# A decode step of cached attention beside a gated MLP: keys in eight-head tiles, values in halves

## The chip, the cores and the metric

The kernel runs on one core of a Trainium2 chip, with nothing on the other cores. The metric is device time in microseconds for one execution, as the median of several runs. A profile of one execution shows where the time goes.

## The reference

One token for each of four batches is normalised; the result feeds an attention over a long cache and a small gated MLP, and both are added to the input.

```python
def _A_ref(x, k_cache, v_cache, wq, wo):      # x: (4, 1, 640); caches: (4, 32, 4096, 128), bf16
    q = (x @ wq).reshape(B, Sq, Hq, Dh).transpose(0, 2, 1, 3)
    scores = jnp.einsum('bhqd,bhkd->bhqk', q, k_cache) * Dh ** (-0.5)
    p = _softmax(scores, axis=-1)
    o = jnp.einsum('bhqk,bhkd->bhqd', p, v_cache)
    return o.transpose(0, 2, 1, 3).reshape(B, Sq, Hq * Dh) @ wo

xn = _layernorm(x, axis=-1)
return x + _A_ref(xn, A_k_cache, A_v_cache, A_wq, A_wo) + _B_ref(xn, B_w_in, B_w_sp, B_b_sp, B_w_out)
```

`_B_ref` projects to 1728 columns, applies gelu, normalises one half, scales and shifts it with `w_sp` and `b_sp`, multiplies by the other half and projects back. The key and value caches are 134 MB each; everything else together is some 14 MB.

## The kernel before

**Tiles.** Work goes tile by tile through the caches. A tile is four heads of one batch: 4 x 4096 rows of 128 numbers, laid over 128 partitions (lanes), so that each lane holds 128 consecutive rows, 32 KB in one run. There are 32 key tiles and 32 value tiles of 4 MB. Eight groups of four heads (`HG`) hold four tiles each, one for each batch.

**Places.** The pool `kv` has five slots of 32 KB a lane. The three first occupants are the two parts of `wq` and the GMLP weights `w_sb`; keys and values then take the slots in the order of the list `loads` (k0, k1, v0, k2, v1, k3, ...). `pump` issues the next loads on SyncE's (SP's) queue when the occupant of the slot five loads earlier is marked as used. The projection weights `wo` have a pool of their own (two buffers, eight blocks of four heads, loaded by `load_wo`; the last in pieces).

**Scores.** A query row is spread over the lanes (`stage_q`). `product(i, half)` multiplies half a key tile by it in place on VectorE (L463); `fold_half` adds the upper 64 columns to the lower (L472); `sums` has TensorE add the 64 columns down to eight through eight matmuls with the identity (L481); `row_sums` (VectorE, L492) adds the eight. Then `lane_max`, `lay_max` (ScalarE), `spread_max` (TensorE), `head_max` and `exps` make the exponents. These five, and `row_sums` of the second half, stand in the next tile's turn, after its first product.

**Values.** The end of `exps` (GpSimd, L539) spreads the probabilities of a tile over the columns of their heads, into one of four `p_m` buffers. `blocks` (L554) multiplies them with the values, 32 matmuls a tile, the two tiles of a pair adding up in `pv_acc`; after the second, ScalarE copies the sum (L564) and `gather` (L575) picks out each head. At the end of a group `group_den`, `group_norm`, `group_turn`, `group_pick` and `group_proj` divide by the denominators and add the group's projection to `out_ps`. The last value tile comes in four pieces, the last three handled by `pairs` (L587).

The order on TensorE, VectorE, ScalarE and SyncE is the order in which the program text is written (`manual_schedule`); GpSimd runs its own list in order. `gmlp` runs whole before the first key tile.

Of the kernel before, what the change touches and what calls it, by code (L numbers as in the profile page):

```python
# [15 lines left out]
KV_SLOTS = 5  # L16
EXTRA_K = (24, 28)
# [4 lines left out]
def kernel(  # L22
# [26 lines left out]
    HT = 4  # L49
# [4 lines left out]
    HC = NC // 2  # L54
    HD2 = Dh // 2
    RW = 8
    SLOT = NC * Dh
# [4 lines left out]

# [5 lines left out]
    kv = ctx.enter_context(tc.tile_pool(name="kv", bufs=KV_SLOTS))  # L68
    wop = ctx.enter_context(tc.tile_pool(name="wop", bufs=2))
# [10 lines left out]
    def slot(name):  # L80
        return kv.tile([P, SLOT], BF16, tag="kv", name=name)


# [4 lines left out]
    wq_v = A_wq.rearrange("(p c) n -> p c n", c=DC)  # L88
    wq_parts = []
    for c0, c1 in ((0, HT), (HT, DC)):  # L90
        t = slot("wq")[:, 0 : (c1 - c0) * HD].rearrange("p (c n) -> p c n", n=HD)
        nc.sync.dma_start(out=t, in_=wq_v[:, c0:c1, :])  # L92
        wq_parts += [(t, i) for i in range(c1 - c0)]
# [6 lines left out]
    w_sb = slot("w_sb")  # L100
    w_in_sb = w_sb[:, 0 : DC * F].rearrange("p (c n) -> p c n", c=DC)
    w_out_sb = w_sb[:, DC * F : DC * F + NFC * D].rearrange("p (k n) -> p k n", k=NFC)
    nc.sync.dma_start(out=w_in_sb, in_=B_w_in.rearrange("(p c) n -> p c n", c=DC))
    nc.sync.dma_start(  # L104
        out=w_out_sb[:, 0:NFF, :], in_=B_w_out[0 : NFF * P].rearrange("(p k) n -> p k n", k=NFF)
    )
    nc.sync.dma_start(out=w_out_sb[:FT, NFF, :], in_=B_w_out[NFF * P : Fh])

    def kv_view(cache, i):
        hg, b = divmod(i, Bsz)  # L110
        return cache[b, HT * hg : HT * (hg + 1)].rearrange("h s d -> (h s) d").rearrange(
            "(p c) d -> p (c d)", c=NC
        )

    k_tiles, v_tiles = {}, {}
    V_CUTS = (0, 64, 96, 112, NC)

    def load(which, i):
        cache, tiles = (A_k_cache, k_tiles) if which == "k" else (A_v_cache, v_tiles)
        t = slot("k_nat" if which == "k" else "v_nat")  # L120
        cuts = V_CUTS if (which, i) == ("v", NT - 1) else (0, NC)
        for c0, c1 in zip(cuts, cuts[1:]):
            if c0 == V_CUTS[1]:
                load_wo(HG - 2)
            nc.sync.dma_start(  # L125
                out=t[:, c0 * Dh : c1 * Dh], in_=kv_view(cache, i)[:, c0 * Dh : c1 * Dh]
            )
        tiles[i] = t[:].rearrange("p (c d) -> p c d", d=Dh)

    loads = [("k", 0), ("k", 1)]  # L130
    n_k = 2
    for i in range(NT):
        loads.append(("v", i))
        for _ in range(2 if i + 1 in EXTRA_K else 1):
            if n_k < NT:
                loads.append(("k", n_k))
                n_k += 1
    occupants = [("w", 0), ("w", 1), ("w", 2)] + loads
    used = set()
    n_loaded = [0]  # L140

    def pump():
        while n_loaded[0] < len(loads):
            at = n_loaded[0] + 3 - KV_SLOTS
            if at >= 0 and occupants[at] not in used:
                return
            load(*loads[n_loaded[0]])
            n_loaded[0] += 1

# [5 lines left out]
    def load_wo(j):  # L155
        wo_tiles[j] = wop.tile([P, HT, D], BF16, name="wo")
        if j == HG - 1:
            for hh in range(HT):
                cuts = (0, D) if hh < HT - 1 else (0, NOH, D)
                for n0, n1 in zip(cuts, cuts[1:]):  # L160
                    nc.sync.dma_start(
                        out=wo_tiles[j][:, hh, n0:n1], in_=wo_h[j][:, hh, n0:n1]
                    )
            return
        nc.sync.dma_start(out=wo_tiles[j][:].rearrange("p r n -> p (r n)"), in_=wo_r[j])

    pump()


# [9 lines left out]
    head_scale = const.tile([P, P], FP32)  # L179
    nc.vector.memset(head_scale[:], 0.0)  # L180
# [7 lines left out]
    for hh in range(HT):  # L188
        ps = slice(hh * LN, (hh + 1) * LN)
        nc.vector.memset(head_scale[ps, ps], scale_qk)  # L190
# [3 lines left out]
    GC = 4  # L194
    CG = P // LN
    assert 2 * GC * HT == LN and GC * Dh * 4 <= 2048
    pv_acc = ps_acc.tile([P, GC * Dh], FP32)
    sel = const.tile([P, GC, HT, 2], FP32)
    for e in range(2):
        nc.vector.tensor_reduce(  # L200
            out=sel[:, :, :, e],
            in_=ident_f[:].rearrange("p (g e k h) -> p e k h g", g=CG, e=2, k=GC)[:, e],
            axis=AX.X,
            op=ALU.add,
        )

    hmask = const.tile([P, HT], FP32)
    nc.vector.memset(hmask[:], 0.0)
    for hh in range(HT):
        nc.vector.memset(hmask[hh * LN : (hh + 1) * LN, hh : hh + 1], 1.0)  # L210
# [7 lines left out]


# [8 lines left out]

    place = const.tile([P, HT, HT * Bsz], BF16)
    nc.gpsimd.memset(place[:], 0.0)  # L230
    for hh in range(HT):
        nc.gpsimd.tensor_copy(
            out=place[:, hh, hh * Bsz : (hh + 1) * Bsz], in_=lane_diag[:, 0:Bsz]
        )
# [5 lines left out]


    p_m = [const.tile([P, NC // GC, LN], BF16, name=f"pm{b}") for b in range(Bsz)]
    acc = [const.tile([P, Bsz], FP32, name=f"acc{g}") for g in range(NACC)]
    for t in p_m:
        nc.gpsimd.memset(t[:], 0.0)


# [25 lines left out]
    for c in range(DC):  # L273
# [5 lines left out]
    xnT = const.tile([P, DC, LN], BF16)  # L279
# [3 lines left out]
    q_sb = const.tile([P, HG // CG, HT * Dh], BF16)  # L283
    q_ps = [
        ps_m.tile([P, HT * Dh], FP32, tag="m", name="q_ps") for _ in range(HG // CG)
    ]
    for c in range(DC):
        t, i = wq_parts[c]
        for hg in range(HG):
            g = hg % CG  # L290
            nc.tensor.matmul(  # L291
                out=q_ps[hg // CG][g * LN : (g + 1) * LN, :],
                lhsT=xnT[:, c, :],
                rhs=t[:, i, hg * HT * Dh : (hg + 1) * HT * Dh],
                start=(c == 0),
                stop=(c == DC - 1),
            )
    nc.vector.tensor_copy(out=q_sb[:, 0, :], in_=q_ps[0][:])  # L298
    nc.scalar.copy(out=q_sb[:, 1, :], in_=q_ps[1][:])

# [26 lines left out]
    def gmlp():  # L329
        zz, gw, gt, gz, sq = (gm[n] for n in ("zz", "gw", "gt", "gz", "sq"))  # L330
        zT = ps_pv.tile([P, 2, NFC, Bsz], FP32, tag="pv", name="zT")
        for t in range(2):
            f1 = t * Fh + NFF * P
            w_t = w_in_sb[:, :, t * Fh : f1].rearrange("p c (f k) -> p c k f", k=NFF)
            for k in range(NFC):
                for c in range(DC):
# [6 lines left out]
                    )  # L343
        nc.vector.tensor_copy(out=zz[:, :, 0:NFF, :], in_=zT[:, :, 0:NFF, :])
# [93 lines left out]
    sums_ps, maxes = {}, {}  # L438

    def stage_q(hg):  # L440
        g, ps = hg % CG, slice(hg % CG * LN, (hg % CG + 1) * LN)
        qr_ps = ps_m.tile([HT * Bsz, Dh], FP32, tag="m", name="qr_ps")
        for hh in range(HT):
# [3 lines left out]
                rhs=q_sb[ps, hg // CG, hh * Dh : (hh + 1) * Dh],  # L447
                start=(hh == 0),
                stop=(hh == HT - 1),
# [11 lines left out]
    def product(i, half):  # L461
        t = k_tiles[i][:, half * HC : (half + 1) * HC, :]
        nc.vector.tensor_tensor(  # L463
            out=t,
            in0=t,
            in1=qbcs[i // Bsz][:, i % Bsz, None, :].to_broadcast([P, HC, Dh]),
            op=ALU.mult,
        )

    def fold_half(i, half):  # L470
        t = k_tiles[i][:, half * HC : (half + 1) * HC, :]
# [4 lines left out]
    def sums(i, half):  # L476
        t = k_tiles[i][:, half * HC : (half + 1) * HC, :]
# [298 lines left out]
```

## Time and profile before

| what | value |
|---|---|
| median of 3 runs | 663.85 us (663.52 to 676.66) |
| profiled execution, its own time | 663.97 us |
| its span in the profile | 662.2 us |
| TensorE, VectorE, ScalarE, GpSimd busy | 53%, 74%, 7%, 23% |
| bytes read from HBM | 282.24 MB, 426 GB/s over the span |
| mean granted TensorE clock | 0.713 |

The profile shows one execution. Its lines give groups of instructions by source line and engine, as busy time, mean duration, and the idle time before them with what ended it. The windows give busy times by stretch of time, with the share of time in which the 16 DMA engines carried packets. Tiles carry the names of the program's buffers.

### The profile page before, as it was taken

Reading aid. Unit: us, or ns where it says so; the run is one execution under the profiler, and the core shown is the slowest. Engines: PE = TensorE matmul, PEld = TensorE weight load, DVE = VectorE, ACT = ScalarE, POOL = GpSimd, SP = SyncE. Lnnn points to the kernel's source line nnn. Section 1 sums busy time; section 2 is a strip of 40 time slices with the busy share of each in tenths; the row PEclk is TensorE's granted clock in tenths of the full one; section 3 lists DMA queues with packets and bytes.
Section 4 is the critical chain, followed back from the end, with each engine's and each line's share of the span. In section 5 each row is a group of like instructions: output and inputs, shape, how many; then the busy total and the mean of one; then the engine's idle time right before and its main releaser. Section 6 shows DMA issues by size and latency. Waiting matters only on the chain.

```text
span 662.2 us, 5116 instructions
## 1 busy us (share of the span) xinstructions
PE 353.6 (53%) x2109; PEld 147.0 (22%) x2109; DVE 491.3 (74%) x334; ACT 49.4 (7%) x138; POOL 151.3 (23%) x57
## 2 busy tenths in 40 slices
PE   2526563646446555664445645465653756435567
PEld 1402221212113221221212212121211312112123
DVE  2289797767769777787776797776787899777950
ACT  0201100001000010001000010000100000000010
POOL 3002222012222012222112222112222133122230
PEclk9999766776755677766778665777576577688586
DMA  9999999999999999999999999999999999999997
GB/s 368 426 416 442 439 418 440 428 434 443 424 431 432 432 442 426 436 430 426 443 428 434 434 424 441 432 431 434 426 438 439 424 442 420 433 443 422 433 430 288
DMA packets 12115, 282.57 MB, mean 427 GB/s; under 512 B 1360, under 2 KB 2108, under 8 KB 3388
## 3 DMA queue, kind: packets, MB, share of 16 engines
q1 hardware_dynamic: 12072, 282.25, 99.2%
q8 instruction: 16, 0.26, 0.1%
q14 instruction: 7, 0.06, 0.0%
q10 hardware_dynamic: 20, 0.01, 0.0%
HBM read 282.24 MB, written 0.01 MB: 426 GB/s over the span
## 4 chain that ended last, share of the span: by engine, by line
issue 49%; DMA 25%; POOL 15%; DVE 7%; PE 3%; SPq 1%; ACT 0%; POOLq 0%; DVEq 0%; ACTq 0%
DMA k_nat<-in_A_k_cache_dram 20%; POOL pm L539 15%; DMA v_nat<-in_A_v_cache_dram 4%; DVE k_nat L463 4%; DVE k_nat L472 2%; PE s_ps L481 2%; PE pv_acc L554 1%; DVE s_sb L492 0%; SPq L125 0%; PE out_ps L653 0%; PE pv L575 0%; SPq L104 0%; POOL own_sum L599 0%; DVE m L501 0%; SPq L92 0%
## 5 line engine op out<-in xcount | busy, mean ns | idle before, releaser
L463 DVE TENSOR_TENSOR k_nat<-k_nat,qbc 128x8192 bf16<-128x8192 bf16 x64 | 282.8, 4419 | 96.2 <-DMA k_nat<-in_A_k_cache_dram 96.2
L539 POOL TENSOR_TENSOR pm<-p,hmask_bf 128x512 bf16<-128x512 bf16 x32 | 142.4, 4451 | 491.7 <-ACT p L530 491.7
L481 PE MATMUL s_ps<-k_nat,ident 128*128 128x512 bf16 x512 | 194.0, 547 | 67.2 <-DVE k_nat L472 67.2
L472 DVE TENSOR_TENSOR k_nat<-k_nat 128x4096 bf16<-128x4096 bf16 x64 | 151.8, 2372 | 0.0
L554 PE MATMUL pv_acc<-v_nat,pm 128*32 128x512 bf16 x1008 | 87.6, 508 | 39.8 <-POOL pm L539 36.2
L514 PE MATMUL max_ps<-lay,head_scale 128*128 128x32 f32 x64 | 19.1, 390 | 167.0 <-ACT lay L507 167.0
L481 PEld LDWEIGHTS <-ident 128*128 128x128 bf16 x512 | 69.7, 138 | 173.8 <-issue 158.8
L514 PEld LDWEIGHTS max_ps<-lay,head_scale 128*128 128x128 f32 x64 | 14.9, 290 | 182.1 <-ACT lay L507 182.1
L554 PEld LDWEIGHTS <-pm 128*32 128x32 bf16 x1008 | 30.0, 118 | 95.8 <-POOL pm L539 52.9
L492 DVE TENSOR_REDUCE s_sb<-s_ps 128x64 f32<-128x512 f32 x64 | 43.3, 677 | 4.3 <-PE s_ps L481 4.3
L507 ACT ACTIVATE lay<-lane_diag,m 128x32 f32<-128x32 f32 x32 | 10.3, 321 | 397.5 <-DVE m L501 397.5
L608 DVE RECIPROCAL rden<-den 128x16 f32<-128x16 f32 x8 | 2.1, 258 | 34.1 <-PE den L606 34.1
L575 PE MATMUL pv<-sel,pv_sb 128*128 128x8 f32 x128 | 20.6, 288 | 8.4 <-ACT pv_sb L564 8.4
L575 PEld LDWEIGHTS pv<-sel,pv_sb 128*128 128x128 f32 x128 | 19.1, 229 | 15.5 <-ACT pv_sb L564 15.5
L530 ACT ACTIVATE p<-s_sb,nb 128x128 bf16<-128x128 f32 x32 | 12.8, 402 | 63.5 <-DVE nb L521 63.5
L564 ACT COPY pv_sb<-pv_acc 128x512 f32<-128x512 f32 x16 | 9.4, 586 | 92.2 <-PE pv_acc L554 92.2
L501 DVE TENSOR_REDUCE m<-s_sb 128x1 f32<-128x128 f32 x32 | 9.1, 286 | 1.1
L291 PE MATMUL q_ps<-wq,xnT 128*32 128x512 bf16 x40 | 4.5, 630 | 8.7 <-DMA wq<-in_A_wq_dram 8.7
L653 PE MATMUL out_ps<-wo,o_r 128*4 128x320 bf16 x56 | 8.1, 437 | 0.0
L298 DVE CAST q_sb<-q_ps 128x512 bf16<-128x512 f32 x1 | 0.7, 692 | 9.7 <-PE q_ps L291 9.7
L613 DVE TENSOR_TENSOR o_n<-pv,rden 128x16 bf16<-128x16 f32 x8 | 1.3, 168 | 7.7 <-PE pv L587 7.7
L521 DVE TENSOR_REDUCE nb<-max_ps 128x1 f32<-128x32 f32 x32 | 5.9, 183 | 0.9 <-PE max_ps L514 0.9
(94 smaller groups left out, 90.4 us busy)
## 6 DMA issues: line engine op xcount, KB each, us to landing
k_nat<-in_A_k_cache_dram SPq DMA_DIRECT2D x32, 4096.0 KB, 37.2
v_nat<-in_A_v_cache_dram SPq DMA_DIRECT2D x31, 4096.0 KB, 33.5
wo<-in_A_wo_dram SPq DMA_DIRECT2D x7, 640.0 KB, 38.3
wq<-in_A_wq_dram SPq DMA_DIRECT2D x1, 4096.0 KB, 13.1
w_sb<-in_B_w_in_dram SPq DMA_DIRECT2D x1, 2160.0 KB, 19.7
v_nat<-in_A_v_cache_dram SPq DMA_DIRECT2D x1, 2048.0 KB, 24.5
wq<-in_A_wq_dram SPq DMA_DIRECT2D x1, 1024.0 KB, 15.0
v_nat<-in_A_v_cache_dram SPq DMA_DIRECT2D x1, 1024.0 KB
```

The costliest lines, as they stand in the source:

```text
L463: nc.vector.tensor_tensor(out=t, in0=t, in1=qbcs[i // Bsz][:, i % Bsz, None, :].to_broadcast([P, HC, Dh]), op=ALU.mult,)
L472: nc.vector.tensor_tensor(out=t[:, :, 0:HD2], in0=t[:, :, 0:HD2], in1=t[:, :, HD2:Dh], op=ALU.add)
L481: nc.tensor.matmul(out=s[:], lhsT=ident[:], rhs=t[:, :, g * RW : (g + 1) * RW], start=(g == 0), stop=(g == n - 1),)
L492: nc.vector.tensor_reduce(out=scores[i][:, half * HC : (half + 1) * HC], in_=sums_ps.pop((i, half))[:], axis=AX.X, op=ALU.add,)
L501: nc.vector.tensor_reduce(out=m1[:], in_=scores[i][:], axis=AX.X, op=ALU.max)
L507: nc.scalar.activation(out=d[:], in_=lane_diag[:], func=ACT.Copy, scale=maxes[i][:, 0:1])
L514: nc.tensor.matmul(out=ps[:], lhsT=head_scale[:], rhs=maxes[i][:], start=True, stop=True)
L530: nc.scalar.activation(out=p[:], in_=scores.pop(i)[:], func=ACT.Exp, bias=nb[:], scale=scale_qk, accum_out=acc[hg % NACC][:, b : b + 1],)
L539: nc.gpsimd.tensor_tensor(out=p_m[b][:, :, e : e + GC * HT].rearrange("p g (c h) -> p g c h", h=HT), in0=p[:].rearrange("p (g c) -> p g c" ...
L554: nc.tensor.matmul(out=pv_acc[g * LN : (g + 1) * LN, :], lhsT=pm[:, c // GC, :], rhs=v_nat[:, c : c + GC, :].rearrange("p c d -> p (c d)") ...
L564: nc.scalar.copy(out=pv_sb[:], in_=pv_acc[:])
L575: nc.tensor.matmul(out=pvs[hg][:, :, b - 1 : b + 1], lhsT=pv_sb[:, k * Dh : (k + 1) * Dh], rhs=sel[:, k, :, :], start=(k == 0), stop=stop ...
```

## The change

A tile becomes eight heads of one batch (`HT = 8`): 256 rows a lane, 64 KB in one run, 16 tiles of keys and 16 of values, four groups. Vector and matrix work on keys goes by quarters (`NQ = 4`), each as large as a half was.

The five slots become one tile, `ring`, of five units of 32 KB. A key tile takes two neighbouring units (a pair, units 2 and 3 for even tiles, 0 and 1 for odd ones) with one load of 8 MB; the first key tile comes in two loads. A value tile comes as two halves of 32 KB a lane: the first goes to the unit of the first half of the same tile's keys, once these are summed, the second to unit 4. The GMLP weights begin in unit 4; their matmuls (`gmlp_in`) stand in the first tile's third quarter, the rest (`gmlp_out`) behind its softmax. For the last three tiles the value halves have other units, written out by hand. The loads stand in a list with their units; `pump` issues the next one when all that was in its units is marked as used, and is called after `sums`, `blocks` and `group_proj`. `wo` has four blocks, one buffer, 10 KB a lane each; the last comes in five pieces after the last values.

The softmax of a tile, from the last `row_sums` to `exps`, stands at the end of its own turn, not in the next (except for the last tile but one). Probabilities are spread by `deal`, twice a tile, 1024 elements a lane each, into one of two `p_m` buffers. `blocks` now runs by halves of a tile: the first half of the tile before in the first quarter of a turn, the second in the third; `gather` follows each tile.

```diff
-    HT = 4
+    HT = 8
-    HC = NC // 2
+    UC = NC // 2
+    NQ = 4
+    QC = NC // NQ
-    kv = ctx.enter_context(tc.tile_pool(name="kv", bufs=KV_SLOTS))
-    wop = ctx.enter_context(tc.tile_pool(name="wop", bufs=2))
+    kv = ctx.enter_context(tc.tile_pool(name="kv", bufs=1))
+    wop = ctx.enter_context(tc.tile_pool(name="wop", bufs=1))
...
+    def load_k(i):
+        t = units(pair(i), 2)
+        step = (1 if i == 0 else 2) * UNIT
+        for e in range(0, 2 * UNIT, step):
+            nc.sync.dma_start(out=t[:, e : e + step], in_=run_view(A_k_cache, i)[:, e : e + step])
...
+    plan_k(0)
+    plan("w", SOLO, 1, load_w)
+    plan_k(1)
+    for i in range(NT - 3):
+        plan_v(i, 0, pair(i))
+        plan_v(i, 1, SOLO)
+        if i % Bsz == 0 and i // Bsz < HG - 1:
+            plan(("wo", i // Bsz), 0, 0, load_wo, i // Bsz)
+        plan_k(i + 2)
+    plan_k(NT - 1)
+    plan_v(NT - 3, 0, SOLO)
+    plan_v(NT - 3, 1, pair(NT - 2))
+    plan_v(NT - 2, 0, SOLO)
+    plan_v(NT - 2, 1, pair(NT - 2) + 1)
+    plan_v(NT - 1, 0, pair(NT - 2))
+    plan_v(NT - 1, 1, SOLO)
+    plan(("wo", HG - 1), 0, 0, load_wo, HG - 1)
...
+    def deal(i, part, engine):
+        g0, g1 = part * UC // GC, (part + 1) * UC // GC
+        engine.tensor_tensor(
+            out=p_m[i % 2][:, g0:g1, :].rearrange("p g (c h) -> p g c h", h=HT),
+            in0=probs[i][:, part * UC : (part + 1) * UC]
+            .rearrange("p (g c) -> p g c", c=GC)[:, :, :, None]
+            .to_broadcast([P, UC // GC, GC, HT]),
+            in1=hmask_bf[:, None, None, :].to_broadcast([P, UC // GC, GC, HT]),
+            op=ALU.mult,
+        )
...
+            for q in range(NQ):
+                product(i, q)
+                if q:
+                    row_sums(i, q - 1)
+                elif late is not None:
+                    row_sums(late, NQ - 1)
+                    lane_max(late)
+                fold(i, q)
+                if q == 0 and late is not None:
+                    exps(late)
+                    deal(late, 0, nc.gpsimd)
+                    deal(late, 1, nc.gpsimd)
+                sums(i, q)
+                if i == 0 and q == 2:
+                    gmlp_in()
+                if i % Bsz == Bsz - 1 and q == 1 and i // Bsz + 1 < HG:
+                    stage_q(i // Bsz + 1)
...
+                elif i:
+                    if q == 0:
+                        blocks(i - 1, 0)
+                    elif q == 2:
+                        blocks(i - 1, 1)
+                        gather(i - 1)
+                        if ends:
+                            group_den(i // Bsz - 1)
+            if ends:
+                group_norm(i // Bsz - 1)
+                group_turn(i // Bsz - 1)
+            if i != LAST - 1:
+                row_sums(i, NQ - 1)
+                lane_max(i)
+                if ends:
+                    group_pick(i // Bsz - 1)
+                exps(i)
+                deal(i, 0, nc.gpsimd)
+                deal(i, 1, nc.vector if i == LAST else nc.gpsimd)
+            if ends:
+                group_proj(i // Bsz - 1)
+            if i == 0:
+                gmlp_out()
+                used.add("w")
+                pump()
```

In the last two turns the `blocks` calls stand elsewhere (the second half of tile 13's values, for one, in the last turn's first quarter), and the last tile's second deal runs on VectorE.

## The prediction, put down before the run

> **What bounds the kernel now.** I read the page's DMA part first, because the diff rewrites the loads, then the windows, the groups by line, and the timelines of VectorE and GpSimd.
>
> ```profile
> span 662.2 us, 5116 instructions
> ...
> DMA  9999999999999999999999999999999999999997
> ...
> DMA packets 12115, 282.57 MB, mean 427 GB/s; under 512 B 1360, under 2 KB 2108, under 8 KB 3388
> ...
> q1 hardware_dynamic: 12072, 282.25, 99.2%
> ```
> ```profile
> 40.00:560.00 520.00, 285.23 (x1529) 114.02 (x1529) 410.82 (x242) 36.23 (x108) 121.76 (x33) 0.69 1.00 433
> ...
> 655.00:658.00 3.00, 1.99 (x65) 1.72 (x64) 0.03 (x1) 0.00 (x0) 0.00 (x0) 0.98 0.74 278
> 658.00:660.00 2.00, 1.27 (x8) 0.50 (x8) 0.62 (x2) 0.42 (x1) 0.00 (x0) 0.50 0.14 42
> ```
> The windows' columns are PE, PE weight load, DVE, ACT and POOL busy, the granted PE clock, DMA share, GB/s. From 40 to 560 us the 16 DMA engines are busy all the time (share 1.00) at 433 GB/s. The chain of waits calls half the span "issue" and puts GpSimd in it, but no engine there is full: the transfers set the pace, and all 282 MB stay in the change. Only three things can move: the transfers' own rate, gaps in the queue, and the ends.
>
> ```profile
> L463 DVE TENSOR_TENSOR k_nat<-k_nat,qbc 128x8192 bf16<-128x8192 bf16 x64 | 282.8, 4419 | 96.2 <-DMA k_nat<-in_A_k_cache_dram 96.2
> L539 POOL TENSOR_TENSOR pm<-p,hmask_bf 128x512 bf16<-128x512 bf16 x32 | 142.4, 4451 | 491.7 <-ACT p L530 491.7
> L481 PE MATMUL s_ps<-k_nat,ident 128*128 128x512 bf16 x512 | 194.0, 547 | 67.2 <-DVE k_nat L472 67.2
> L472 DVE TENSOR_TENSOR k_nat<-k_nat 128x4096 bf16<-128x4096 bf16 x64 | 151.8, 2372 | 0.0
> L554 PE MATMUL pv_acc<-v_nat,pm 128*32 128x512 bf16 x1008 | 87.6, 508 | 39.8 <-POOL pm L539 36.2
> L492 DVE TENSOR_REDUCE s_sb<-s_ps 128x64 f32<-128x512 f32 x64 | 43.3, 677 | 4.3 <-PE s_ps L481 4.3
> ```
> ```profile
> 90.78 4.41 DVE L463 TENSOR_TENSOR k_nat<-k_nat,qbc 128x8192 bf16<-128x8192 bf16 x1
> 95.11 0.68 DVE L492 TENSOR_REDUCE s_sb<-s_ps 128x64 f32<-128x512 f32 x1
> 95.71 2.52 DVE L472 TENSOR_TENSOR k_nat<-k_nat 128x4096 bf16<-128x4096 bf16 x1
> 102.88 4.43 DVE L463 TENSOR_TENSOR k_nat<-k_nat,qbc 128x8192 bf16<-128x8192 bf16 x1 [4.65 <-DMA k_nat<-in_A_k_cache_dram]
> ```
> ```profile
> 630.71 4.56 POOL L539 TENSOR_TENSOR pm<-p,hmask_bf 128x512 bf16<-128x512 bf16 x1 [10.37 <-ACT p L530]
> 644.49 1.04 POOL L539 TENSOR_TENSOR pm<-p,hmask_bf 128x512 bf16<-128x512 bf16 x1 [9.22 <-ACT p L530]
> ```
> VectorE waits for keys between tiles (4.65 us in the last DVE line). The same GpSimd multiply takes 4.56 us beside a running product and 1.04 us at 644.49, where VectorE is idle: its own work is 1.04 us, the rest is waiting for the product to end.
>
> **Part 1, the transfers (-1.2 us).** The trace's DMA packet records give one engine's packet as 1.213 us for 32 KB, 0.611 for 16 KB, 0.309 for 8 KB, 0.196 for 5,120 B. These lie on one line: 602 ns for each 16 KB and 9 ns a packet. A 64 KB key run is then 9 + 2408 = 2.417 us against 2 x 1.213. Each engine carries 8 lanes of each of the 16 key tiles: 128 pairs x 9 ns = 1.15 us saved. The nearest other row, a run cut into two packets all the same, saves 0. Projection weights: 7 blocks of 8 x 0.196 plus a last one in 1280 and 640 byte pieces (1.83) were 12.8 us; 3 of 8 x 0.385 plus a last one twice as large (3.66) are 12.9. `wq` in one 40 KB run, values in 32 KB runs: the same. Half the key issues on SP's queue fall away; SP is idle, nothing. I take -1.2.
>
> At this place a rule speaks for much more. The Trainium skill, page "DMA: Bandwidth & Descriptors" (Anatomy of one DMA), puts a fixed cost of some 2 us on each DMA beside its bytes. The trace does not show that cost here: with transfers queued behind one another the share is 1.00 at 433 GB/s. By the page 16 fewer key DMAs would take off some 32 us (an estimate), by the row nothing; it stands as a rival.
>
> **Part 2, the start (0).** Order on the queue: `wq` 12.1 us, first key tile 2 x 9.70, GMLP weights 7.8, second key tile 19.35, then values into the first tile's freed half. The slowest engine starts at about 3.5, so that values end at 3.5 + 12.1 + 19.4 + 7.8 + 19.35 + 9.7 = 71.9, or 72.7 with the 0.8 that the first key transfer lost beside those weights now. The next half needs the place of the GMLP weights, freed when `gmlp_out` is done. First keys at 25.6; four quarters of product 4.42, row sums 0.65 and fold 2.28 (the first without row sums) are 28.8, giving 54.4; sums 3.57, row sums, maximum, exponent, about 6 us, give 60.6; the GMLP chain took 8.1 us (25.26 to 33.40) and pays one more table load, 1.28: 70. First packets follow an issue by 1.0 us (0.74 to 1.77 at the start), 71 against 72.7: no gap. If the GMLP's small products wait for both deals, 2 to 4 us, the gap is up to 2.
>
> **Part 3, the ring (+0.3; bounds 0 and 27).** Five 32 KB places remain, but a key tile now claims two at once. Keys i+1 may only be issued when `blocks(i-1, 0)` has read the values in their first place. From the last packet of keys i: landing 0.35, product and fold 6.7, sums 3.03 (194.0/64), `blocks` 2.74 (87.6/32), issue 1.0: packets can flow at 13.8 to 14.1 (the values themselves land at 10.05), and the queue holds work until 19.4. So 5 us in hand; with both matmul groups at their slow 3.57 and 3.61, 4.2.
>
> The second question is whether a tile's chain fits into the period of 2 x 19.4 = 38.8 us. Before, the softmax of a tile lay under the next tile's first product; now `row_sums(i, 3)` to `exps(i)` run ahead of it, and VectorE waits: sums of the third quarter 21.4 to 24.4, `blocks` to 27.2, copy and gather 0.59 + 1.06, last sums to 31.9, then 0.65 + 0.41 + 0.33 + 0.63 + 0.2 = 34.1, exponent 34.7, both deals. A deal has 1024 elements a lane instead of 512: 2.08 us at twice the 1.04, lower bound 1.04, upper 4.56, the common row. 1.04 is its nearest row, since VectorE is idle just then. 35.1 + 2 x 2.08 = 39.2 against the next keys at 39.1: they just fit, and one product in some periods starts late by a microsecond, inside the 5 us. At the slow matmul durations the same chain ends at 41.2: 2.1 us a period if deals go first, 13 periods, 27 us; that is the upper bound. The mean rows are the ones that a mixed clock (0.69 in the window) gives, so I take 0.3, for one or two slips. Group ends (tiles 4, 8, 12) add den, turn and pick, 1 to 1.5 us; the 3.1 us of projection weights lie ahead of the key load after two of them.
>
> **Part 4, the end (+1.7; bounds 0 and 6).** The last packet lands at about 658.7 now and the span ends 3.5 later. In the new order the last tile's product starts some 51.6 before the last packet (behind the late values of tile 13): quarters 29.7, two deals in the windows 4, last sums 3.03, softmax 2.9, deal 2.1 and denominator 0.9 give -7.4 or so; `blocks` 2.74, half of it again, copy and gather 1.7, pairs 2.1, norm 0.4, sixteen projections 2.5: +2.5. Result copy and output 2.7: 5.2 after the last packet instead of 3.5. All matmuls fast: 0; all slow: +6.
>
> **Sum.** 662.2 - 1.2 + 0 + 0.3 + 1.7 = 663.0. The profiled execution took 663.97, 1.8 over its span; the median of three is 663.85, so the execution stands for it. 663.0 + 1.8 = 664.8.
>
> **Rivals.**
> *The run is still two packets* (the change does not do what it says): the saving of 1.2 is gone, 666.0. No packet in the trace is over 32 KB, so nothing speaks against it. Chance 0.08.
>
> *The ring runs dry, slower.* Place: the deals at the end of tile i against the first product of tile i+1. Once the two deals end over 4 us after the next keys landed (a deal over 3.5 us, or half clock throughout), keys i+1 come late each period. For it: L539's common 4.56 and matmul groups of 3.57; against: 1.04 without a product, and products that never exceed 4.43 now. Price: about 1 us x 14 periods, + 6 at the end - 1.2 = +19, 683. Chance 0.14. The Trainium skill, "SBUF — State Buffer" (Who interferes with whom), calls that shared port an exclusive lock held for the whole instruction; 4.56 against 1.04 agrees, and by it a deal that comes first holds up the whole product, 2.08 each.
>
> *Values read with gaps.* Halves of 32 KB now lie 64 KB apart in memory. If that slowed them to the 417 GB/s of the slowest early window (20 to 40 us) instead of 433, 134.2 MB take 321.8 instead of 309.9: +12, 677. Against: 32 KB packets are at 1.213 in nine of ten records. Chance 0.04. The Trainium skill, same DMA page (Latency and other measured facts), has a row pitch of 512 KiB cost some 3%; no run here shows a pitch beyond 32 KB.
>
> *A fixed cost per DMA goes* (the rule in part 1): 16 x 2 is the page's estimate; by rows a cost can hide only in the gap of 433 and the 443 of the best slices, 2.3% of 655: 15 us, 649. Chance 0.01, as share 1.00 speaks against it.
>
> **Numbers.** My forecast has 0.73, its own range 661.5 to 669. The range to 676 takes in the split run and the ring's milder slips; under 661.5 would need an end shorter than today's. Over 2% (about what a measurement of this kernel can tell from no change, 650.6 and 677.1) slower: the ring 0.13, half of the values 0.02, together 0.15; faster 0.01; within 0.84.
>
> **What would show it.** Right: key packets of 64 KB, share 1.00 and 433 GB/s in the middle, products waiting for keys and never SP's key issue for `blocks` while the queue is empty, deals near 2 us, and 5 us from last landing to the end. Wrong: DMA digits under 9 at a period of about 40 us, or `pm` rows of 4 us and more at tile ends, would give the ring; a middle under 430 GB/s at share 1.00 the spaced values. Above 677 or below 651 the reading "transfers set the time" is wrong.

## The result, and the profile after

The changed kernel takes 670.13 us (median of 6, 668.78 to 672.55) against 663.62 us for the kernel before (median of 6, three of them those of the table above): a ratio of 1.0098, 95% interval 1.0087 to 1.0109. It is slower by 6.5 us, 5.3 us above the predicted 664.8, and within the 2% that was named as no difference. It lies above the forecast's own range (661.5 to 669) and inside the wider one, to 676, that took in milder slips of the ring. The profiled execution is the quickest of the six, 668.78 us with a span of 666.8; the other five have spans of 667.3 to 670.5.

The page's head, DMA rows and queue:

```profile
span 666.8 us, 4747 instructions
...
DMA  9999899999999999999999999999999999999997
...
DMA packets 9873, 282.56 MB, mean 424 GB/s; under 512 B 1040, under 2 KB 2428, under 8 KB 2812
...
q1 hardware_dynamic: 9832, 282.25, 98.6%
```

The bytes are the same, in 2242 fewer packets, 1920 of them by key runs of 64 KB, but the share fell from 99.2% to 98.6% and one digit, the fifth (67 to 83 us), is below 9. The windows (PE, weight load, DVE, ACT and POOL busy, granted clock, DMA share, GB/s) show where:

```profile
71.00:73.00 2.00, 0.64 (x6) 0.14 (x3) 2.00 (x1) 0.00 (x0) 0.00 (x0) 0.50 0.87 250
73.00:557.00 484.00, 226.37 (x1396) 89.03 (x1399) 377.74 (x183) 21.75 (x55) 70.28 (x27) 0.69 1.00 432
557.00:560.00 3.00, 1.39 (x24) 0.55 (x17) 3.00 (x3) 0.00 (x0) 0.00 (x0) 0.95 1.11 382
560.00:618.00 58.00, 27.88 (x132) 10.31 (x132) 52.99 (x25) 1.80 (x5) 7.92 (x2) 0.68 0.97 417
618.00:620.00 2.00, 0.70 (x4) 0.34 (x4) 2.00 (x3) 0.55 (x2) 0.00 (x0) 1.00 0.86 279
```

The middle runs as before, 432 GB/s at share 1.00. Three short stretches do not: 71 to 73, 557 to 560 and 618 to 620 us. (A window counts a packet whole if it starts there. So in a short one the share can pass 1, and 560 to 618 us shows only 417 GB/s although the packet records have no gap between 561 and 616.) From the start and length of each packet in the trace's DMA records, the 16 engines stand idle, on the mean, 1.42, 1.64 and 0.35 us in the three; the packets around them run long by another 0.60, 0.69 and 0.44. That is 5.1 us. Less the 1.2 us that the longer runs were to save, and with 0.3 more at the end (last packet 662.98, end 3.8 behind it; before 658.68 and 3.5), 4.2 of the 4.6 us between the two spans are placed; the other 0.4 is spread thin. Some 0.2 to 0.3 us more lie outside the span: an execution of the changed kernel takes 1.98 to 2.12 us over its span, one of the kernel before 1.73 to 1.85.

**The first stretch.** The timeline there:

```profile
61.46 3.74 POOL L561 TENSOR_TENSOR pm<-p,hmask_bf 128x1024 bf16<-128x1024 bf16 x2 [52.18 <-ACT gt L380]
61.50 1.90 DVE L383 TENSOR_SCALAR gt<-gt 128x56 f32<-128x56 f32 x1 [0.32 <-ACT gt L380]
63.44 1.84 DVE L386 TENSOR_TENSOR gz<-zz,gt 128x56 f32<-128x56 f32 x1
69.61 2.03 PE L456 MATMUL out_ps<-ring,yT 128*4 128x320 bf16 x14 [0.92 <-DVE yT L452]
71.68 0.33 SPq L139 DMA_DIRECT2D ring<-in_A_v_cache_dram  x1
```

Two steps of the GMLP's gelu on VectorE take 1.90 and 1.84 us, each as long as one of the two deals that GpSimd runs beside them. The GMLP weights are read for the last time at 71.6, and the second half of the first values, which takes their place, is issued at 71.68. By then most of the 16 engines have run dry, from 70.9 us on; the new packets start at 72.6 to 73.5.

**The second stretch.** VectorE's waits (total, times, longest) and its timeline through tile 12:

```profile
DVE ring L495 <- DMA ring<-in_A_k_cache_dram: 46.2, 11, 6.2
DVE s_sb L527 <- PE s_ps L513: 43.3, 15, 3.7
DVE rden L626 <- PE den L624: 26.1, 4, 8.5
```
```profile
501.90 4.43 DVE L495 TENSOR_TENSOR ring<-ring,qbc 128x8192 bf16<-128x8192 bf16 x1 [5.86 <-DMA ring<-in_A_k_cache_dram]
506.36 2.29 DVE L504 TENSOR_TENSOR ring<-ring 128x4096 bf16<-128x4096 bf16 x1
508.57 4.42 DVE L495 TENSOR_TENSOR ring<-ring,qbc 128x8192 bf16<-128x8192 bf16 x1
...
530.50 0.36 DVE L626 RECIPROCAL rden<-den 128x32 f32<-128x32 f32 x1 [7.58 <-PE den L624]
530.78 4.36 DVE L495 TENSOR_TENSOR ring<-ring,qbc 128x8192 bf16<-128x8192 bf16 x1
...
543.87 4.42 DVE L495 TENSOR_TENSOR ring<-ring,qbc 128x8192 bf16<-128x8192 bf16 x1
548.32 3.86 DVE L504 TENSOR_TENSOR ring<-ring 128x4096 bf16<-128x4096 bf16 x1
552.11 6.11 DVE L495 TENSOR_TENSOR ring<-ring,qbc 128x8192 bf16<-128x8192 bf16 x1
```
```profile
496.81 3.74 POOL L561 TENSOR_TENSOR pm<-p,hmask_bf 128x1024 bf16<-128x1024 bf16 x2 [33.94 <-ACT p L550]
544.73 9.21 POOL L561 TENSOR_TENSOR pm<-p,hmask_bf 128x1024 bf16<-128x1024 bf16 x2 [43.97 <-ACT p L550]
580.18 7.92 POOL L561 TENSOR_TENSOR pm<-p,hmask_bf 128x1024 bf16<-128x1024 bf16 x2 [26.24 <-ACT p L550]
```

At a group end the reciprocal of the denominators, 0.36 us of work, stands ahead of the last product in VectorE's list, and its matmul stands behind `blocks` and `gather` on TensorE: VectorE stands still for 7.58 us. Tile 12 started on time (it had waited 5.86 us for its keys), but tile 13's product starts 42.0 us later, not 38.8. By then the deals of tile 12 no longer fall into the gap between tiles: they meet tile 13's first product and take 9.21 us instead of 3.74. By their times in the trace each waits for the one before: the first deal ends 1.7 us behind that product, the fold behind the first deal, the second deal behind the fold, the second product behind the second deal. Fold and product take 3.86 and 6.11 us instead of 2.28 and 4.42. The same happens behind the other two group ends (pairs of 9.21 us at 227.57 and 386.50). The tile after each is still late (7.92 us, the last row); at the other tile ends up to tile 11 the pair takes 3.74 or 3.75.

How far this delays the next transfer is read from what the key load waits for. The key loads behind tiles 12 and 13, and on TensorE the sums and `blocks` ahead of the second:

```profile
514.50 0.33 SPq L131 DMA_DIRECT2D ring<-in_A_k_cache_dram  x1
```
```profile
552.24 3.57 PE L513 MATMUL s_ps<-ring,ident 128*128 128x512 bf16 x8 [6.18 <-DVE ring L504]
555.74 2.65 PE L575 MATMUL pv_acc<-ring,pm 128*32 128x512 bf16 x32
558.45 0.33 SPq L131 DMA_DIRECT2D ring<-in_A_k_cache_dram  x1
```

Tile 14's keys wait for `blocks` to read the first half of tile 12's values, and that stands behind the sums of tile 13's first quarter. They are issued 43.95 us after tile 13's keys, 5.2 over the period: 3.2 from the late start, 1.6 from the held fold, 0.4 from a slower `blocks`. The held second product lies behind all this and adds nothing. The ring had some 5 us in hand for the slowest DMA engine, but the engines end their work up to 2 us apart: all but a few have run dry between 556.6 and 558.5 us, and the new packets start at 559.4 to 560.2.

### The profile page after: what moved, and what is told of

Same layout as the page of the kernel before. It is cut to its first block, busy times and chain, and to the rows that moved or that the text cites. A ratio compares the mean times of both kernels' runs of the same rounds, so it can differ in the third digit from the quotient of the medians.

```text
span 666.8 us, 4747 instructions
## 1 busy us (share of the span) xinstructions
PE 313.4 (47%) x2033; PEld 127.2 (19%) x2033; DVE 507.4 (76%) x278; ACT 34.3 (5%) x82; POOL 97.9 (15%) x60
## 3 DMA queue, kind: packets, MB, share of 16 engines
q1 hardware_dynamic: 9832, 282.25, 98.6%
## 4 chain that ended last, share of the span: by engine, by line
DMA 48%; DVE 34%; PE 17%; ACT 1%; issue 1%; SPq 0%; DVEq 0%; ACTq 0%
DMA ring<-in_A_k_cache_dram 41%; DVE ring L495 19%; DVE ring L504 11%; PE s_ps L513 10%; PE pv_acc L575 5%; DMA ring<-in_A_v_cache_dram 3%; DMA wo<-in_A_wo_dram 3%; DVE s_sb L527 2%; PE zT L363 1%; PE pv L593 0%; DVE gt L383 0%; PE max_ps L540 0%; DVE gz L386 0%; ACT pv_sb L589 0%; DVE m L536 0%
## 5 line engine op out<-in xcount | busy, mean ns | idle before, releaser
L495 DVE TENSOR_TENSOR ring<-ring,qbc 128x8192 bf16<-128x8192 bf16 x64 | 291.7, 4558 | 46.2 <-DMA ring<-in_A_k_cache_dram 46.2
L513 PE MATMUL s_ps<-ring,ident 128*128 128x512 bf16 x512 | 187.9, 533 | 284.0 <-DVE ring L504 284.0
L561 POOL TENSOR_TENSOR pm<-p,hmask_bf 128x1024 bf16<-128x1024 bf16 x31 | 93.5, 3035 | 548.6 <-ACT p L550 496.4
L504 DVE TENSOR_TENSOR ring<-ring 128x4096 bf16<-128x4096 bf16 x64 | 156.6, 2447 | 0.5
L513 PEld LDWEIGHTS <-ident 128*128 128x128 bf16 x512 | 63.9, 126 | 385.5 <-issue 320.0
L575 PE MATMUL pv_acc<-ring,pm 128*32 128x512 bf16 x1008 | 77.4, 462 | 0.9 <-DMA ring<-in_A_v_cache_dram 0.9
L540 PE MATMUL max_ps<-lay,head_scale 128*128 128x16 f32 x32 | 7.0, 294 | 23.4 <-ACT lay L538 23.4
L540 PEld LDWEIGHTS max_ps<-lay,head_scale 128*128 128x128 f32 x32 | 5.4, 211 | 30.6 <-ACT lay L538 30.6
L550 ACT ACTIVATE p<-s_sb,nb 128x256 bf16<-128x256 f32 x16 | 8.1, 508 | 12.3 <-DVE nb L546 12.3
L536 DVE TENSOR_REDUCE m<-s_sb 128x1 f32<-128x256 f32 x16 | 6.7, 420 | 0.5
```

What stands on the lines that cost most here:

```text
L495: nc.vector.tensor_tensor(out=t, in0=t, in1=qbcs[i // Bsz][:, i % Bsz, None, :].to_broadcast([P, QC, Dh]), op=ALU.mult,)
L504: nc.vector.tensor_tensor(out=t[:, :, 0:HD2], in0=t[:, :, 0:HD2], in1=t[:, :, HD2:Dh], op=ALU.add)
L513: nc.tensor.matmul(out=s[:], lhsT=ident[:], rhs=t[:, :, g * RW : (g + 1) * RW], start=(g == 0), stop=(g == n - 1),)
L536: nc.vector.tensor_reduce(out=m1[:], in_=scores[i][:], axis=AX.X, op=ALU.max)
L540: nc.tensor.matmul(out=ps[:], lhsT=head_scale[:], rhs=d[:], start=True, stop=True)
L550: nc.scalar.activation(out=p[:], in_=scores.pop(i)[:], func=ACT.Exp, bias=nb[:], scale=scale_qk, accum_out=acc[hg % NACC][:, b : b + 1],)
```

## The experiments

The theory: three causes, each with its place. The deals beside the GMLP (start), the wait for the denominators (group ends), and an end that hangs on TensorE's clock. The rivals: that the 64 KB runs or the 8 MB loads cost by themselves, and that the places, not the order of work, are too few.

**The GMLP's rest ahead of the first softmax.**

```diff
+            if i == 0:
+                gmlp_out()
+                used.add("w")
+                pump()
             if i != LAST - 1:
                 row_sums(i, NQ - 1)
...
-            if i == 0:
-                gmlp_out()
-                used.add("w")
-                pump()
```

> Edit: in the first tile's turn gmlp_out (the rest of the GMLP) stands before the tile's last row_sums and softmax instead of behind its deals. Theory A (the 4.6 us of span over the kernel before are local: 2.4 at the start, 2.3 at the key load of tile 14 behind the third group end, 0.8 at the first values of tile 14, 0.3 at the end, less 1.2 saved by 64 KB runs): the two deals no longer hold up the GMLP's small VectorE work, its weights' place is free before the values ahead in the queue have landed, and the dip in the DMA share at 71 to 73 us goes: 2.0 to 2.6 us shorter than the changed kernel, median about 667.7. Rival B (a key tile in one 8 MB load keeps the queue too short everywhere; the start is one dip of many): under 0.7 us shorter, the lost time comes back at the next tile's key load. Rival C (packets of 64 KB, or values 64 KB apart, move more slowly): no change.

Measured: 672.13 us (4 runs, 668.02 to 672.83), 1.0117 of before, 1.0086 to 1.0148. A miss: the expected 2 us did not come. The interval takes in that of the changed kernel, so no loss is shown either. The step itself did what it was to do. Its windows and timeline:

```profile
71.00:73.00 2.00, 0.23 (x1) 0.10 (x1) 2.00 (x2) 0.00 (x0) 2.00 (x1) 0.50 1.10 475
557.00:560.00 3.00, 1.27 (x4) 0.45 (x4) 3.00 (x2) 0.00 (x0) 0.00 (x0) 0.69 0.82 284
616.00:620.00 4.00, 3.21 (x30) 1.33 (x26) 4.00 (x3) 0.84 (x3) 1.08 (x1) 0.98 0.65 225
```
```profile
55.11 0.19 DVE L383 TENSOR_SCALAR gt<-gt 128x56 f32<-128x56 f32 x1 [0.31 <-ACT gt L380]
```

The gap at 71 us is gone and the gelu step is back at 0.19 us. Tile 12 starts 2.2 us earlier (499.67 against 501.90). Then the time is given back. The second stretch stays and comes 2 us earlier (idle 1.51 us from 554 on); a short new one stands at 577 (idle 0.22, packets long by 0.64); and 616 to 620 moves 225 GB/s (336 in the changed kernel), idle 1.48 us instead of 0.35. What opens the last two wider is not shown. Tile 14's second value half lands no earlier (640.71, the changed kernel's 640.07), and this profile ends 30.0 us after its last packet, the changed kernel's 26.7. The deals moved, too: tile 0's pair now meets tile 1's first product and takes 9.20 us, at no cost that shows. Of the theories this is nearest to rival B, though the loss comes back at the last tiles and not at the next key load. Here a gap closed early, with others behind it, was no gain by itself.

**The denominators early.** `group_den` moves to the third quarter, ahead of `fold`.

```diff
+                if ends and q == 2:
+                    group_den(i // Bsz - 1)
                 fold(i, q)
...
                         gather(i - 1)
-                        if ends:
-                            group_den(i // Bsz - 1)
```

> Edit: group_den stands in the third quarter ahead of fold, so that its matmul lies behind the second quarter's sums on TensorE instead of behind blocks and gather. Theory A: the 26.1 us in four times that VectorE waits for den in the changed kernel (7.4 to 7.6 at each of the three group ends inside the ring) fall under 3 in those three, the tiles after the group ends start on time, and the key load of tile 14 is issued ahead of the end of the queue: 2 to 4 us shorter, median 666 to 668. Rival B (the slack of the ring is too short at every tile): the wait goes but the time stays within 1 us. Rival C: no change.

Measured: 668.03 us (4 runs), 1.0065, 1.0042 to 1.0089: 2.1 us better, at the lower edge of what was expected; with 4 runs the interval still touches that of the changed kernel. The wait is gone, and with it two of the three stretches:

```profile
DVE rden L626 <- PE den L624: 2.7, 1, 2.7
```
```profile
71.00:73.00 2.00, 0.00 (x0) 0.00 (x0) 2.00 (x1) 0.00 (x0) 0.00 (x0) 0.50 0.88 279
557.00:560.00 3.00, 0.00 (x0) 0.00 (x0) 3.00 (x3) 0.00 (x0) 0.00 (x0) 0.76 1.11 475
616.00:620.00 4.00, 2.37 (x36) 1.21 (x35) 4.00 (x3) 0.58 (x1) 4.00 (x1) 1.00 1.03 438
```

Only the last wait is left, at the end of the kernel. The pairs of deals behind the group ends take 3.74 us again. The second and the third stretch run at full rate; the first, which has another cause, stays.

**Keys in two loads of 4 MB.** The same places, the run cut in two.

```diff
-        step = (1 if i == 0 else 2) * UNIT
+        step = UNIT
```

> Edit: every key tile comes in two loads of 32 KB a lane instead of one of 64 KB, all else as changed. Theory A: the run costs 9 ns a packet more, 1.15 us in all, but a tile's first product may begin 9.7 us earlier, so that the dips at tile 14 go while the start's stays: 1 to 2.5 us shorter, median about 668. Rival B (the 8 MB load with its one landing is what starves the queue): 4 to 6 us shorter, median at or under 665, the dip at the start smaller too. Rival C (packets of 64 KB are slow in themselves): the DMA time over the ideal of 1.213 a 32 KB packet falls from 3.9 us per engine to 2, and 2 us are won with the dips still there.

Measured: 667.57 us (4 runs), 1.0063, 1.0038 to 1.0087: 2.6 us better, though it gives back the packets saved; the 4 to 6 us of rival B did not come. No gap is left but the first (1.03 us). With the first half of the keys landed half a transfer earlier, the product has some 9.7 us more in hand, and the group ends fit. They fit although nothing in the order of work was mended. VectorE still waits for the denominators, and from tile 1 to tile 13 every pair of deals runs beside products, for 8.65 or 9.21 us (tile 13's is shown):

```profile
DVE rden L626 <- PE den L624: 20.3, 4, 5.9
```
```profile
575.89 9.21 POOL L561 TENSOR_TENSOR pm<-p,hmask_bf 128x1024 bf16<-128x1024 bf16 x2 [26.25 <-ACT p L550]
```

So neither the wait nor the collision of deals and product costs a transfer by itself. They cost one when the turn has nothing left in hand, and the one landing of a whole key tile, half a transfer later, is part of what took it away.

**The projection weights one tile later.** They are 3.1 us of transfer that lie ahead of the key load after the group ends of tiles 4 and 8; tile 12 has none.

```diff
-        if i % Bsz == 0 and i // Bsz < HG - 1:
+        if i % Bsz == 1 and i // Bsz < HG - 1:
```

> Edit: the three early projection blocks are loaded one tile later (behind the values of tiles 1, 5 and 9 instead of 0, 4 and 8), so that the key loads right behind the first two group ends lose the 3.1 us of transfers ahead of them. Theory A: these two key loads then come late as that of tile 14 does, some 2.3 us each: 3 to 5 us longer, median 673 to 675, with two new dips of the DMA share near 245 and 403 us. Rivals B and C: the bytes and the number of loads are the same, no change beyond 1 us.

Measured: 674.45 us (4 runs), 1.0166, 1.0149 to 1.0183, where 673 to 675 was expected. New stretches stand at 241 to 243 and 401 to 404 us, idle 0.91 and 1.02 us with packets long by 0.60 and 0.69, the key loads behind the ends of tiles 4 and 8. So every group end is late, and the changed kernel shows one gap of three only because weights cover two. Smaller ones, which had not been expected, stand at 80 us (idle 0.30 us), where tile 0's weights had been, and at 580 (0.40), and the one at 620 grows from 0.35 to 0.98.

**The last values later.** `blocks` and `gather` of tile 14's second half go behind the last softmax, so that the last sums do not wait for those values.

```diff
-                    elif q == 2:
-                        blocks(i - 1, 1)
-                        gather(i - 1)
...
         assert not loads
+        blocks(LAST - 1, 1)
+        gather(LAST - 1)
         group_den(HG - 1)
```

> Edit to the changed kernel: in the last turn the second half of tile 14's values and its gather are multiplied behind the last tile's softmax, not ahead of its last sums. Theory D (the end is a chain that starts when these values land: blocks, copy, gather, last sums, softmax, deals, the last tile's blocks; it took 26.2 us in the changed kernel's profile and 29.7 to 30.3 in three of the experiments, by the matmul clock, while the transfers left after that landing take 22.9, with 3.5 for the output behind them): 3 to 5 us leave the chain, the transfers set the end again at some 26.4 after the landing, the median falls by 1.5 to 3.5 and the runs lie closer together: 667 to 668.5. Rival E (the end is set by the projection weights, which land last, in every run): no change.

Measured: 670.24 us (4 runs), 1.0096, 1.0083 to 1.0110: no gain, a miss for the median. But the spans, 666.8 to 670.5 in the changed kernel, are 668.0 to 668.3 here: over four runs the end no longer varies. In the one profile it hangs on the transfers, with the last packet at 664.18 and the end 3.8 later; the last packet itself comes 24.5 us after tile 14's values, not 22.9, and why is not shown.

**Start and denominators together** (the first two edits).

> Both earlier edits at once: gmlp_out ahead of the first softmax, group_den ahead of the third quarter's fold. Theory A with D: no dip of the DMA share from 3 us to the last values, the last packet at about 657.5 us instead of 663, but the end stays a chain of about 30 us from the landing of tile 14's second half (634.5): span 662 to 665, median 664 to 667. Rival B (the ring is too short at every tile): dips remain after tiles without a group end, median 668 and more.

Measured: 665.89 us (10 runs), 1.0027, 1.0013 to 1.0041, as expected. No gap is left from 3 us to the last values. Of the 6.5 us lost in the medians, 4.2 are back: 2.1 by the denominators, and now 2.1 by the start, which alone had brought nothing.

**All repairs.** The two, the late values, the first `blocks` of tile 13 moved ahead of the last sums of tile 14, and the last tile's deals exchanged (the first on VectorE, the second on GpSimd), with the last denominators behind its first `blocks`:

```diff
+                if i == LAST - 1 and q == 3:
+                    blocks(i - 1, 0)
                 sums(i, q)
...
                 elif i == LAST - 1:
-                    if q == 3:
-                        blocks(i - 1, 0)
+                    pass
...
-                deal(i, 0, nc.gpsimd)
-                deal(i, 1, nc.vector if i == LAST else nc.gpsimd)
+                deal(i, 0, nc.vector if i == LAST else nc.gpsimd)
+                deal(i, 1, nc.gpsimd)
...
         assert not loads
+        blocks(LAST - 1, 1)
+        gather(LAST - 1)
+        blocks(LAST, 0)
         group_den(HG - 1)
-        blocks(LAST, 0)
```

> Both edits, tile 14's late values behind the last softmax, the first half of tile 13's values ahead of tile 14's last sums, and at the very end the first deal on VectorE, the second on GpSimd, with the denominator behind the first blocks. Theories A and D: transfers set the time from 2 us to the end; last packet 657.3, 3.5 to the end, span 660.8, 662.6 to 663.0, that is 0.6 to 1.0 under the kernel before: the 1.2 us of the 64 KB runs come out at last. Rival B: over 665. Rival C (packets of 64 KB or spaced values are slower): 664 to 665 with no dips.

Measured: 664.34 us (12 runs), 1.0014, 1.0002 to 1.0025. A miss by 1.5 us: 0.6 behind the kernel before (663.70) and not 0.6 to 1.0 ahead of it. Seven of the twelve spans lie at 661.1 to 662.2, five at 663.1 to 665.4. The kernel before has 27 of 29 spans at 661.5 to 662.9 and two at 666.4 and 666.5, so the spread is new.

**All repairs, keys in two loads.**

> As the kernel with all repairs, but each key tile in two loads of 32 KB a lane. With the transfers as the bound this measures the run length alone: 128 more packets an engine at 9 ns, 1.15 us longer than the other (663.8 to 664.2, level with the kernel before). If instead the one landing of 8 MB costs time, it is as fast or faster.

Measured: 664.90 us (12 runs), 1.0013, 0.9994 to 1.0032. The expected 1.15 us for the cut run is not told apart: the medians differ by 0.56, less than the spread of either. The two loads show no gain any more once the group ends are repaired. One difference is clear of the spread: the time over the span is 1.72 to 1.85 us here and 2.10 to 2.29 in the kernel with all repairs. It is so in every pair of this case: 1.72 to 1.89 in each run with key loads of 4 MB, the kernel before among them, and 1.97 to 2.29 in each with loads of 8 MB. So some 0.3 us of what the longer runs save inside the span is lost outside it; why, no run shows.

**Second profiles of the repaired kernels**, to see what the spread is made of.

> The kernel with all repairs once more, for a second profile. Its twelve times fell into two clusters, spans of 661.1 to 662.2 us and of 663.1 to 665.4; the profile at hand is of the second (663.8) and shows 2.5 us of packet time above the usual between 40 and 65 us, while the projection weights and the second key tile load. Theory A (the upper cluster is slow packets in the early loads, a matter of the execution): a profile with a span near 661.3 shows under 0.5 us of excess there, one near 663.8 shows 2 us or more. Theory B (the upper cluster is TensorE's clock in the last 27 us): the early excess is 2 us in either, and the difference lies between the last landing of values and the end.

> The kernel with the first two repairs once more, for a second profile; the one at hand has a span of 665.2 us, an early excess of 0.3 us and 30.2 us from the landing of tile 14's second value half (634.97) to the end. Theory A (its spread of 661.1 to 665.3 is the tail's matmul clock): a profile near 661 to 662 has 26 to 27 us in that tail, one near 665 has 30. Theory B (the spread comes from slow packets or gaps ahead of it): the landing itself moves by 3 us and the tail stays at 30.

One time each: 667.10 and 665.80 us, spans 664.9 and 663.7. The windows from 40 to 65 us, first and second profile of all repairs, then of start and denominators:

```profile
40.00:65.00 25.00, 17.15 (x140) 9.03 (x138) 18.48 (x29) 3.98 (x7) 0.00 (x0) 0.64 1.03 399
```
```profile
40.00:65.00 25.00, 16.70 (x139) 8.67 (x138) 19.33 (x30) 4.18 (x8) 0.29 (x1) 0.70 1.02 433
```
```profile
40.00:65.00 25.00, 17.87 (x140) 9.34 (x139) 19.00 (x30) 4.03 (x8) 0.00 (x0) 0.50 1.02 434
```
```profile
40.00:65.00 25.00, 17.24 (x140) 8.99 (x139) 18.87 (x30) 4.14 (x8) 0.00 (x0) 0.57 1.02 397
```

One profile of each kernel has slow early packets (399 and 397 GB/s, 25 x (1 - 398/433) = 2.0 us), one has not. And the end comes in two forms:

| profile | early GB/s | last packet of tile 14's second values | span | from one to the other |
|---|---|---|---|---|
| all repairs | 399 | 636.78 | 663.8 | 27.0 |
| all repairs, second | 433 | 634.52 | 664.9 | 30.4 |
| start and denominators | 434 | 634.62 | 665.2 | 30.6 |
| start and denominators, second | 397 | 636.96 | 663.7 | 26.7 |
| changed kernel | | 640.07 | 666.8 | 26.7 |

So neither theory holds alone. For all repairs both fail: the slower span had no slow packets, against A, and the early excess is in one profile and not in both, against B. For start and denominators the tail does take 26.7 and 30.6 as A said, but the landing moves by 2.3 us as well, which B said. The spread is the two together: 634.6 + 26.7 = 661.3 is the best case, seen in spans of 661.1 and more; with one of the two losses 663.7 or 665. With both it would be 667, which none of these 24 spans reaches. In the 26.7 form the transfers set the end: the last packet is 22.9 after tile 14's, the end 3.8 later (4.1 in the first profile of all repairs). In the 30.4 form the last packet of the second profile of all repairs lands at 657.44, and the end is 7.4 later: TensorE sets it. Its rows there, and then those of the first profile:

```profile
644.91 3.60 PE L575 MATMUL pv_acc<-ring,pm 128*32 128x512 bf16 x32
...
651.07 3.41 PE L575 MATMUL pv_acc<-ring,pm 128*32 128x512 bf16 x32
...
659.59 2.30 PE L671 MATMUL out_ps<-wo,o_n 128*4 128x320 bf16 x16 [0.28 <-DVE o_n L631]
```
```profile
647.62 3.27 PE L575 MATMUL pv_acc<-ring,pm 128*32 128x512 bf16 x32
...
652.63 1.91 PE L575 MATMUL pv_acc<-ring,pm 128*32 128x512 bf16 x32
...
659.54 1.25 PE L671 MATMUL out_ps<-wo,o_n 128*4 128x320 bf16 x16 [0.28 <-DVE o_n L631]
```

The same 32 matmuls (second row) take 3.41 or 1.91 us, the same 16 projections 2.30 or 1.25. The granted clock in 650 to 655 us is 0.58 in the one and 0.96 in the other. What makes the early packets slow in some executions, and what sets the clock in the tail, stays open; no run here turned either on or off. Both slow-packet profiles had the quick end, but two are too few to tie them together.

## Why the prediction was right or wrong, point by point

**What bounds the kernel: right.** The middle stays at 432 GB/s and share 1.00, and nearly all that was lost is a stretch where the queue was empty, or the end.

**Part 1, transfers, -1.2: right in size.** A 64 KB packet takes 2.418 us in the records (2.417 was worked out). The first key tile comes in two loads, so it is 15 loads and 120 pairs an engine, not 16 and 128; with all packets at their usual lengths an engine has 1.1 us less to do. So the run is not split, and the rivals "still two packets", "read with gaps" and "a fixed cost per DMA" fall: the value packets stay at 1.213 us, the middle keeps its rate, and with half the key loads nothing but that 1.1 went. The section of the Trainium skill that the prediction cites for the fixed cost, "DMA: Bandwidth & Descriptors" (Anatomy of one DMA), is about DMAs issued from GpSimd; these are issued from SP. Against "read with gaps" the working said that no run had a pitch beyond 32 KB; `wq`, in two parts, already had 40 KB.

**Part 2, the start, 0: wrong by 2.0.** The term that failed is the GMLP chain at "8.1 us" from the trace of before, where GpSimd was idle beside it; from its first copy to its last matmul it now takes 11.4, 3.3 more. The slowest DMA engine ran dry at 72.3, inside the 71.9 to 72.7 worked out, but most of the others a microsecond before it. The sentence behind the sum had the right cause and the right bound ("if the GMLP's small products wait for both deals ... the gap is up to 2") but it was left out of the sum. They do wait for both: 1.90 and 1.84 us in place of 0.19 and 0.22, which is the 3.3 us; 1.28 had been allowed for a table load. The Trainium skill, "SBUF — State Buffer" (Who interferes with whom), says that whoever issues first has the shared ports for its whole instruction; these rows agree, and here it is GpSimd that holds up VectorE.

**Part 3, the ring, +0.3: the step that failed.** The hand of 5 us and the fit of the chain into the period were right for ordinary tiles: a pair of deals is 3.74 (2 x 2.08 was taken) and tile 12 still waited 5.86 us for its keys. The mis-sized term is "Group ends ... add den, turn and pick, 1 to 1.5 us". They add 7.58 + 0.36 + 1.2 = 9.1 us, of which the 5.86 of waiting absorbs part and 3.2 remain. On the way to the next key load the collision of deals and product adds 1.6, and `blocks` 0.4. The working counted instructions and not the place of `group_den` in the two lists. The profile of before had it in its waits view, at no cost then, as the transfers never stopped:

```profile
DVE rden L608 <- PE den L606: 34.1, 8, 6.2
```

The sentence on the weights ("ahead of the key load after two of them") was right, and moving them showed it, but the third end was then taken as covered. The 5 us in hand were counted for the slowest DMA engine, and the mean one had less. Price: 1.64 + 0.69 at 557 us, and 0.35 + 0.44 at 618, which go with the same edit; 3.1 in the profile, 2.1 in the medians.

**The rival "ring runs dry"** named the right collision, deals against the next product, and the wrong place: not each period, but only behind a group end, where the turn was already late. So 3 us and not 19. Its sign, `pm` rows of 4 us and more, is there at six tile ends; the run with keys in two loads has it at 13 in a row and shows no gap from it, so it is a sign of deals that meet a product and not of a loss.

**Part 4, the end, +1.7 (bounds 0 and 6): 0.3 in the profiled execution, inside the bounds.** "5.2 after the last packet" is 3.8 where the transfers set the end, as they do in this profile, and 7.1 to 7.7 in profiles of five of the experiments, where TensorE does. The working had one chain at mean matmul durations, and so missed that the end has two forms. Its terms do not add up either: those listed give -9.0 and not -7.4, then +1.8 and not +2.5, and 4.5 in all, that is +1.0. That 1.7 lies near the middle of what the executions show is luck. The span of the profiled execution plus the 3.7 between the forms is the 670.5 of the slowest span; the median of the times lies 1.35 above the profiled one. That this is the end's long form is argued, as the changed kernel has one profile.

**The sum.** The 1.8 us over the span were carried over from the kernel before; they are 2.0 to 2.1. In the profiled execution -1.2, +2.0, +3.1, +0.3 gives 4.2 of the 4.6 us. The median stays within the wider range because the two terms taken as nearly nothing, the start and the group ends, cost 5.1 us together, and not because they had been seen.

## What to carry to other kernels

When a change takes slack out of a ring of places, read the waits of each engine's list that cost nothing today: an instruction of 0.36 us that waits for a result far back in another engine's list is free while there is slack; here it stopped VectorE for 7.6 us and made the turn 3.2 us late when the slack was gone. Count what stands ahead of a step in both lists, not only its own time, and look for the one turn in four that differs. Where transfers set the pace, a gap repaired may show in the time only when the gaps behind it are repaired too, as the start did here.

## What had not been expected of the hardware

- A VectorE step on 128 x 56 numbers took 1.90 us instead of 0.19 beside a GpSimd deal; a pair of deals took 3.74 us alone and 9.21 beside products, and the fold and the product beside it 3.86 and 6.11 for 2.28 and 4.42. The hold goes both ways.
- The same deal takes 1.23 us on VectorE (the last tile's) and 1.87 on GpSimd alone.
- Packets between 40 and 65 us ran at 397 to 399 GB/s in two profiles and at 433 to 434 in two others of the same two kernels.
- The time of an execution over its span in the profile was 1.72 to 1.89 us in every run with key loads of 4 MB and 1.97 to 2.29 in every one with loads of 8 MB.
